# Two blocks of a layer pair on one core: new hand-laid queues, and 64x64 products that lie across the halves of two PSUM banks

## The chip, the core and the metric

The kernel runs on one core of a Trainium2 chip. Its time is that of the device in microseconds (us). Times that are compared are medians of several executions; a profile is of one execution, and has a time of its own.

## What is computed

The input is 2048 tokens of 512 features in bf16. Two kinds of block alternate, A B A B, each added to its input:

```python
def _A_ref(x, wqkv, wo):      # H = 32 heads of 16, window W = 256
    qkv = (x @ wqkv).reshape(B, S, 3, H, Dh)
    scores = einsum("bhqd,bhkd->bhqk", q, k) * Dh ** -0.5
    mask = (i - j >= 0) & (i - j < W)
    return einsum("bhqk,bhkd->bhqd", softmax(where(mask, scores, -1e9)), v) @ wo
def _B_ref(x, w1, b1, w2, b2):     # mixes tokens: F = 1792
    u = gelu(einsum("bsd,sf->bdf", layernorm(x), w1) + b1)
    return einsum("bdf,fs->bds", u, w2) + b2
x = x + _A_ref(_layernorm(x), A_wqkv, A_wo)
x = x + _B_ref(_layernorm(x), ...)        # and both once more
```

## The kernel before

**Stages.** A "layer" below is one A and one B; there are two. The attention of a layer is cut into four quarters Q of 512 queries, and a quarter into four groups t of 8 heads, and these into 9 steps m: 144 steps a layer, 288 in all. In a step TensorE multiplies scores (`emit_scores`, L753), ScalarE takes exp from two PSUM banks (`emit_exp`, L765, into one of ten slots of `p_all`), VectorE or GpSimd masks the window's edges (`mask`, L795), and TensorE multiplies with v (`emit_pv`, L816). Scores have two pairs of PSUM banks (0-1, 2-3) in turn, the sums with v have banks 4 and 5. After the ninth step the sums are copied out of banks 4 and 5 into `oU` and `o2` (`copy_out`, L374 on VectorE, L376 on ScalarE). After each second group two DMAs move rows of `o2` into `oU`, and two move the softmax denominators into `den_c`, so the next copy into `o2` waits for DMAs of the groups before. `job_inverse` and `job_normalise` (L842 to L867) divide, `job_outproj` (L726) multiplies with wo and adds to x.

**Work beside the attention.** The products with wqkv (`job_kq`, `job_v`), with wo, a part of the first product of B (`job_u_part`) and, in the first layer, twelve of the sixteen tiles of B's second product (`job_y_pair`) are put between the steps of attention. All go through `pair`, which makes two products at once in the two "misc" banks 6 and 7. Three kinds of work share these banks: pairs, `job_normalise`, and some of B's products. The bank of each use is read from the string `BANKS`. A digit of the string `CELLS` says how `pair` makes the two: 0 is each product as matmuls of 128x128 weights and 512 columns (L559), and 1 is both at once in four 64x64 tiles of TensorE (L573); then row half r works on product r, and on the other one in the second half of the pass, so that the row halves never write one bank at the same time. The attention's own matmuls are all 64x64 tiles. A stretch of 128x128 matmuls between 64x64 ones is called an island here.

**The rest of B** lies between the attentions: `u_product` and `job_u` (L944), `job_y` (L1035, L1022), with layer norm (`ln_stats` L488, `ln_apply` L508 to L520). Transposed inputs `xhT` (two buffers in turn) of the quarters after the first come by DMA transposes that SyncE issues (`job_transpose`, L535).

**Order.** `Plan.op` records each piece of work with its reads and writes, and so its dependencies. The order on each engine was searched off line and is written out: `ORDER` names, two letters an operation, what TensorE, VectorE, ScalarE, GpSimd and SyncE each run, one after the other. `arrange` reads it, lets users of one misc bank follow each other in TensorE's order, and `needs` sets the waits. Each engine runs its list strictly in order, SyncE (the DMA queue) too: what waits holds all that is behind it.

```python
        for b in sorted({int(s) for s in self.stays}):
            used = [self.res["bank", s].users for s in self.stays if int(s) == b]
...
            a, b = misc_bank(), misc_bank()
            pairs.append((a, b))
            if CELLS[len(pairs) - 1] == "0":
                for i, bank in enumerate((a, b)):
                    for lo, hi in pieces or ((0, n),):
```

Without `pieces`, a product of four matmuls is one operation, so nothing comes between its matmuls.

Of the kernel before, what the change touches and what calls it, by code (L numbers as in the profile page):

```python
# [7 lines left out]
ALU = mybir.AluOpType  # L8
# [7 lines left out]
CELLS = '000001000000110001001110000001000000000000000000000000000000001100000101000000'  # L16
# [13 lines left out]
        ApAqArAsAtBEAuBGAvBKBIBOBMBQBSAwAxB4CXCUBkCfCcDRCoCTClC2BlCuDAAyC8CeCkDLCnCtC1DGCyDZC7DVCxDhC-DEDIDeBuDmDrBvD5DPDYD8DSEH  # L30
        DdDgEKE+ERDlDqEUD4D7EAEjEmDuErEvDvEJEQETEiE5ElEqEuE0EzEYFVE2FCFxFdE9FaFpFyFiFBF2FUFZFtEZGDFcFhGAFoFsF1F5GPGlGHGCGZGLGWGG
        GOGVGhGYGcGdGmGxGgGpGqG+G7GuG4GKHPG-HJG3HXH3HTH4HmG6HIHjHOHSHzG0HWHiHlHwHpIEI8IBHyH2INIDIJHLIKIMIQItIRHaI2HbIxIcIwJBIVI6
        IzJIIUJFI9JYJMKvJiJcI5JnJjJAJxJEJHJLJ0JXJbJmJ4JqKAJ7KHJ8KKJzJ3J-KOKGKJKSKwKbKNKRKgMWKnKaKdKsLoK6LpLAKmKrLEK5KXLILUKWLXMX
        LhK-LDLkLHLTKjLyLWLaL1MQL5LjL8MPMALnL0MML4L7K8MUL-MLMTMdNJMaMhMsMjMwMkMzMgMrM3MvMyM2NDMDNHMENSNCNGNNNdNWNgLLNlLMNoNfNvNK
        NyNkN6ObN+MnNnOHOCNuNxN5N9OBOVN1OOOEOkN2OZONOUOYOuOjOoOpORO1OtOyMoPCOxO0O-OcPRO4PONPPePBPNPWOQPnPQPjNOP6PVPdP0PiOKPmPrQB
        P3P+PaQJPZQFP9QAQbQEOfQOQIQNQaQeRbQfQgPFPGRVRYPsPtRZRhRcQqReRiRfQtRSRTQ5QxRgQ4QwRWRURPRQRMRRRNRORoRXRmRqRaR0R1RdRsRwSARk
        RuSBR4SISESJR8R9R5SFRjRySwTtTuSxSmTvSnSrSsShSiTwTpTqTrTsUXS9UYTDUZS-UaTBTGTFTJTdTlTKUbT7T+UcUdUDUGUeThUTT9ULTiTTUyUCUFUK
        U2USUxU7TUU1U6VAU9VKUPVNUOVSVVVHVaVEVMVfVRVUVtVZVeVsVwVjV7VvV0V+WGVGWYWVWHWIWqWnWJWCWvWzV9WUWXWmWpW4WuWyW3W9WDWEW6XJXGWF
        ViXrXOXCXBXwXFXIX1XNXqXvX0X4X5XUYBYCYMWcXVYPYTX+XWYbYFYiXXX9YlYpYOYSYaYhYkYoYtXQY2YsZJY1ZGXRXSZTZQXTYxZPZSZnZhYWYXZrZgZm
        ZvWdZ7ZqZuZ6Z9Z+aBaIY8aLYyY9ayaKavY+Y-a5aka2Y4Y5a9bJY6Y7bNaxa1bSa4ZMbWa8bIbMbPbdZWbhbVbcbkZjbgbjbobnbYbZbzb3b0aOaPaQaRcB  # L40
        cAb4aSZXcLcOcEaTaUaVZycccUbBcYcmcjalb9b8cNcqZzcTcuc3cbcXc8ciclcpdDctc2c5dGbAdUdCdcamdgdFdTdkdJdwdbdfdjdzdKdvdyd9eAd2cyeO
        czeRd-eDeVeQeUeYeEeeeXeqeFeuezc-edepete3ewe+e5fefFe2fCe6fVe9fBfJg2fofEfZgLf2fIfUfzfYfhfsf+fdf7gIgMgFf1gUg3gQf6f9gEgdgHdW
        gYgPgTgXgtgagkdog8gjgxehhGgsgwhBdnhNhKeihag7hAhXhFgghJhMhphQhmh4hZhlhohthugmgnh9h3iBh8goiOgpiAiUiFiYiRfifjibiffkflijiXia
        ioieiiini1gzi0i4jvi5i6iGhzh0hej1hdj7iHjsjEj4jwjyjHj2j8jTjSj5jLjKjzjthxjmjnhyj3jojukIjpj9j+jxj0kGkCjqkijrkjkWkAkMkSkTkekf
        kEkOkPkXkakbj6kKlClGk2k3lDlHk6k7lOlSlPlTlelflalmlblql2lrlyl3lnlzlulvl6mFl7l+l-mC
    """,
    "vector": """
        A2ASATAQA3ARA0A1AUAVA8AWA6A4A7A5A+BAA-AXBFBDBCBUBJBYBZBaBRBWBVBXBbB8BcBeCWBmBoDTCVBqBnCaBrCrBjIfBtIdFGDDC0CzFEBsDKDbBxDp
        FIByIgFKDUIhFAECEWFHB1EoFJFFIjFLDxIiB2IeFMB3FOIkDyDzEyEaE3FzFXE-D1F0FrD2FSInFkFgF4EcF6F7EbGFFTEdGnIlGNGSGjEfGoHAGvGwGMHB
        HCHDHEGzHFH5H6HGHVG1G2HrHqI+IGHHHMHNH7H8H9ITHcHfHdH+I1IZIaIWI-IXKxHgHeIYHhIbJRKzJlJPJkJ2JrJsKCJ9K1KMJ+KDKUKyMYKeKfK2LqK3  # L50
        KuLrKZLsLGKEKYMZLZLuKlLbLcKkL3MSMRK+K9LvMONLMcMbMlMmLwM5MIMFMGNXNYMJLQLNMHLONMLRLPN0LSMKN8M8NrM6OdOAM+M-OFOGN3N4OwNsOTOr
        MqO6O5NROeOSPgNQPlOLP4OMP5PcPbQLOhQQOgQhPKPHQnPIPuPvPxQrPwQsPyPLPJPMPzQRQuQTQvQYQWQVQ9Q1Q+Q2Q6QyQ7Q3QzQ0Q-Q8RCRARGRER2SC
        SKR+R6SGSySzSoS0SpSqStSuSjSkSvSlS3S1T0TxTyS+TETATCUfTIT5UgTNTMTQUAToUhTST6UiUIUnUJUoTzTRUpTkUrUVTVTXUWTWU+U4URUQU5VXVJVc
        VdTZVhTaVyVlV1VIWNWbWsW-W8WKXLVkVmXMXDXzVoUvVpWSYEYAYRWTYGYHX-XbWLYrYeZHXgXYWMZVXhXZWgXaXkXiYYYZWiZtWhWfaCaDWjY0YfaNYga0
        WkWlXpZDZAbLZEZBZFZObQbRZNZkZlZabmbbaWaXcDZCZdcGcFaZaaZ0abaYaebFbGacceb-b+cfcoZ3cgapcZc6c7Z1bCaqaoZ2asdiZ4Z5bHbDdmbEbrdL
        aud3btd4d1dNc0c1dPdOdQeGeHegdRdAdBeIexe7bwfge8fAg4byfLfqgNftfuffgAgOg5gBgSdYdXgbgcdseLgCejekgDdtdueldpdqemendreofOfMghhc
        hSgifRfQfTeMhrh6iDeNh-gqiSiTiWidfnfmilg0iqg1i8i7iIh2hijBhjiJhfiLiKjFhgjGjIjJiMiNjXhhhkirjUitivjPjQjMjVjYjNjOjWjZjRjajcjh
        kkkUkQkYkgkclIlEk8k4lglUlclQlol0lwl4mGlsl8mAmD
    """,
    "scalar": """  # L60
        AaBHAcAbAdAzBLBPBNBTAlB5CYAfCgCdCpAoCmC3CvDBC9DMDHDaDWDiDfDJDnDsBwD6D9EIELESEVEkEnEBEwDwEsE6E1FWFDFeE4FbFqFjF3FuGEGBGQGI
        GaGXGiGeGyGrGTG8G5HQHKHYHUHnHkH0HxIFICIOILIuISI3IyJCI7JJJGI0JNJZJdJoJyJ1J5KBKIKLKPKTKcKhKoKtK7LBLFLJLVLYLiLlLzL2L6L9MBMN
        MVMeMiMtMxM0M4NENINTNeNhNmNpNwNzN7N-MpOIODOWOPOlOaOvOqO2OzPDPAPSPPPfPXPoPkP7P1QCP-QKQGQcQPRIQiQoQXRFRHRnRrRvRtR3RpRlRxSL
        SDR-R7SHRzS6SYS7THTLTeTmT8T-UHUETjUMUUUzU3U8VBVLVOU-VTVWVbVgVuVxV-V8TbWZWWV2WoWrWwW0W5W+XKXHW7XPXsXEXxX2X6YDYNWeYQYUYcYj
        YmYqYuZKY3ZIZUZRYzZiZoZsZwZ8Z-aJaMXnazawa6a3a+bKbObTbXbeZYbiblbpbab1cCb5ZZcPZfcMcdcVcaanckcncrcvc4c9dEdHdVdddhdldxd0dMd+
# [12 lines left out]
        FnO7O9O8OsPYO+NVOiOnPUQjQkKqSaPhQZRKQmQlSNIHSOQHRLSQPqNjP2QMSPRJKpSSSZSeSRSMSbSfSdSgUNScSTT2T1UkUjT3TgUlVFTfT4V3V6V4UmV5
        YIWPYLYKYJWQWOWRaEXeXcXfaFaGXdaHYVYwX8X7cHcKcIcxcRcJcSb7cWb6d5d8d6d7ecfvebfyfwfxhThVg-hWhUdZhEg6hwh7hsi+i9iEjji-frfbjAkm
        kqjkjlf5fcdak0kxizkvimk1kniQkzkrihkwkokskuktkpk9lMlLkylAk-lVk+lKlWlJljk5ldlXlYlhlklilBlNl5lZlRlxlllplFltl1l9mBmHmE  # L80
    """,
}
BANKS = (
    "7667766776766767666677767767666767767666677667677767767667676767677667676776766767767667677766677777"
    "7767766767766767776776676777667666676776676667776767767667677667776776667767666776677776676667676767"
    "7677"
)
# [24 lines left out]
class Plan:  # L112
# [52 lines left out]
    def arrange(self):  # L165
# [119 lines left out]
def bass_interleave_layers__sliding_block__mixer_token_mlp__prompt_kernel(  # L285
# [11 lines left out]
    S = A_x.shape[1]  # L297
# [12 lines left out]
    with es:  # L310
# [216 lines left out]
        def misc_bank():  # L527
            stays.append(Bank(BANKS[len(stays)]))
            return stays[-1]

# [18 lines left out]
        def pair(make, n, prio, reads, pieces=None):  # L549

            a, b = misc_bank(), misc_bank()
            pairs.append((a, b))
            if CELLS[len(pairs) - 1] == "0":
                for i, bank in enumerate((a, b)):
                    for lo, hi in pieces or ((0, n),):
# [8 lines left out]
            for half in range(2):  # L564
                for lo, hi in pieces or ((0, n),):
# [14 lines left out]
            return a, b  # L580

# [34 lines left out]
        def store_k(Q, t, b, prio):  # L616
            masked(b, prio, k_sb[:, Q % 2, t].rearrange("p b (h n) -> p b h n", h=2), ps[:, b, :].rearrange("p (b n) -> p b n", n=32),
                   half, "half", [R("k", Q % 2, t, hf) for hf in range(2)], 1226, 1230)

        def store_q(Q, t, b, prio):  # L620
            masked(b, prio, q_sb[:, t].unsqueeze(1), ps[:, b, :].unsqueeze(1), even, "even", [R("q", t)], 1226, 1230)
# [44 lines left out]
        def job_v(Q, i, prio):  # L666

            a, b = pair((w_half(Q, 2, 2 * i), w_half(Q, 2, 2 * i + 1)), 4, prio, w_held(2, 2 * i) + xhT_all(Q))
            for j, bank in enumerate((a, b)):
                copy_out(vT[:, j, :], ps[:, bank, :], bank, prio, 691, [R("vT", j)])  # L670
                plan.ops[-1].deps = dict.fromkeys(plan.ops[-1].deps, 0)
# [510 lines left out]
```

## Time and profile before

| | |
|---|---|
| median of 3 runs | 494.68 us (494.25 to 495.84) |
| the profiled execution | 493.93 us, its span 492.2 us |
| granted TensorE clock | 1.0 in every slice |
| attention of the first layer | from 13.71 us to about 155 us |
| B of the first layer | to about 229 us |
| attention of the second layer | 229.19 us to about 390 us |
| B of the second layer | to 488.9 us |
| busy in 60 to 80 us | PE 17.66, DVE 16.54, ACT 19.36, POOL 13.95 of 20 |
| busy in 420 to 440 us | PE 19.89, DVE 4.04, ACT 8.21, POOL 0 of 20 |

Times in the profile count from the start of the span. PE is TensorE's matmuls, PEld its weight loads, DVE VectorE, ACT ScalarE, POOL GpSimd, SP SyncE. A row of the timeline gives start, length, engine, line, operation, tiles and number of instructions merged, and in brackets how long the engine was idle before and who ended it. Some matmul records are missing: of an island of four, often three are shown.

### The profile page before, as it was taken

The numbers are of one execution on the slowest core, as the hardware profiler recorded it, in microseconds if no ns is written. First come the engines' busy times: TensorE is split into PE (matmuls) and PEld (weight loads), VectorE is DVE, ScalarE is ACT, GpSimd is POOL, SyncE is SP. The second block draws the span as 40 slices with busy tenths as digits, with TensorE's granted clock in tenths as the row PEclk, the third lists the DMA queues.
The fourth block names the chain that finished last, engine by engine and source line by source line (L and its number), as shares of the span: only waits on it lengthen the run. The fifth ranks groups of instructions, "written<-read, shape, count | busy, mean of one in ns | idle before, by whom it ended". The sixth has DMA issues, their size and how long they took to land.

```text
span 492.2 us, 17751 instructions
## 1 busy us (share of the span) xinstructions
PE 465.4 (95%) x7966; PEld 260.5 (53%) x8042; DVE 327.1 (66%) x623; ACT 316.2 (64%) x389; POOL 197.3 (40%) x270
## 2 busy tenths in 40 slices
PE   7999997999999999999999999999999999999997
PEld 6545563766655444443555556456557644444444
DVE  6999997998966741346856776689996674022213
ACT  3999997999997013306898899699999602330000
POOL 5998975736553100013654444286643003000000
PEclk9999999999999999999999999999999999999999
DMA  7231542603105980301510342062023497022553
GB/s 212 90 46 49 110 93 46 92 11 43 49 20 140 280 225 9 99 0 44 119 47 3 101 107 41 15 99 49 3 50 81 113 265 215 1 85 62 153 150 128
DMA packets 85180, 43.63 MB, mean 89 GB/s; under 512 B 19953, under 2 KB 84081, under 8 KB 85105
## 3 DMA queue, kind: packets, MB, share of 16 engines
q1 hardware_dynamic: 81232, 42.48, 33.7%
q0 software_dynamic: 3872, 0.02, 1.3%
q8 instruction: 63, 1.03, 0.9%
q14 instruction: 13, 0.10, 0.1%
HBM read 32.51 MB, written 2.10 MB: 70 GB/s over the span
## 4 chain that ended last, share of the span: by engine, by line
PE 58%; DVE 11%; ACT 11%; DMA 6%; POOL 5%; SPq 4%; issue 3%; DVEq 0%; POOLq 0%
PE ps L559 17%; PE ps L1035 12%; ACT p_all L765 10%; PE ps L944 10%; PE ps L753 8%; PE ps L816 6%; DMA oU<-o 4%; PE ps L573 3%; SPq L368 3%; DVE stats L488 2%; POOL p_all L795 2%; DVE q_sb L607 1%; POOL xh_sb L517 1%; SPq L535 1%; DMA k_sb<-in_B_w_dram 1%
## 5 line engine op out<-in xcount | busy, mean ns | idle before, releaser
L765 ACT ACTIVATE p_all<-ps 128x1024 bf16<-128x1024 f32 (+8 forms) x288 | 260.0, 974 | 21.2 <-PE ps L753 19.2
L795 POOL TENSOR_TENSOR p_all<-p_all,edge 128x512 bf16<-128x512 bf16 (+3 forms) x125 | 97.9, 790 | 102.9 <-ACT p_all L765 98.5
L753 PE MATMUL ps<-q_sb,k_sb 64*64 64x288 bf16 (+8 forms) x2816 | 107.1, 249 | 2.1 <-ACT p_all L765 1.6
L816 PE MATMUL ps<-p_all,v_all 64*64 64x288 bf16 (+8 forms) x2816 | 86.6, 246 | 1.2 <-DVE p_all L795 0.6
L753 PEld LDWEIGHTS ps<-q_sb,k_sb 64*64 64x64 bf16 x2816 | 56.1, 106 | 52.9 <-ACT p_all L765 32.5
L559 PE MATMUL ps<-xhT,wqkv 128*128 128x512 bf16 x281 | 73.4, 380 | 9.9 <-issue 4.0
L816 PEld LDWEIGHTS ps<-p_all,v_all 64*64 64x64 bf16 x2816 | 58.7, 107 | 10.1 <-issue 3.3
L1054 DVE SCALAR_TENSOR_TENSOR x_sb<-ps,b2col,x_sb 128x512 bf16<-128x512 f32 x31 | 22.7, 746 | 56.4 <-PE ps L1035 46.5
L559 PEld LDWEIGHTS ps<-xhT,wqkv 128*128 128x128 bf16 x320 | 25.9, 97 | 38.3 <-issue 4.6
L510 POOL TENSOR_TENSOR rstd<-vare,mhalf 128x4 f32<-128x4 f32 x15 | 15.3, 1022 | 76.5 <-DVE vare L508 73.4
L488 DVE BATCH_NORM_STATS2 stats<-x_sb 128x6 f32<-128x512 bf16 x64 | 42.8, 681 | 4.1 <-DMA x_sb<-in_A_x_dram 3.6
L559 PE MATMUL ps<-uT,w1buf 128*128 128x512 bf16 x157 | 39.0, 380 | 1.5 <-issue 1.4
L520 ACT ACTIVATE xh_sb<-x_sb,shift,rstd 128x512 bf16<-128x512 bf16 x9 | 7.1, 809 | 51.7 <-POOL shift L514 51.7
L656 POOL TENSOR_TENSOR v_all<-vB,evens 128x512 bf16<-128x512 bf16 x29 | 33.9, 1172 | 14.5 <-DVE vB L674 13.9
L607 DVE TENSOR_TENSOR q_sb<-ps,even 128x1024 bf16<-128x1024 f32 x29 | 35.1, 1213 | 5.7 <-PE ps L559 5.5
L795 DVE TENSOR_TENSOR p_all<-p_all,edge 128x128 bf16<-128x128 bf16 (+3 forms) x87 | 29.6, 345 | 12.8 <-ACT p_all L765 11.5
L607 DVE TENSOR_TENSOR k_sb<-ps,half 128x1024 bf16<-128x1024 f32 (+1 forms) x28 | 33.4, 1194 | 2.0 <-PE ps L559 1.5
L1035 PE MATMUL ps<-uT,oU 128*128 128x512 bf16 x151 | 34.4, 379 | 0.2
L1007 DVE TENSOR_TENSOR v_all<-v_all,ps 128x512 f32<-128x512 f32 x12 | 8.2, 687 | 39.3 <-PE ps L944 39.3
L944 PE MATMUL ps<-xh_sb,k_sb 128*128 128x512 bf16 x124 | 30.0, 379 | 1.6 <-DMA k_sb<-in_B_w_dram 0.9
L867 DVE TENSOR_TENSOR oT<-oU,ps 128x512 bf16<-128x512 f32 x32 | 21.2, 680 | 9.7 <-PE ps L860 7.5
L559 PE MATMUL ps<-wo_sb,oT 128*128 128x512 bf16 x99 | 24.9, 380 | 1.2 <-issue 0.6
(98 smaller groups left out, 543.6 us busy)
## 6 DMA issues: line engine op xcount, KB each, us to landing
w1buf<-in_B_w_dram SPq DMA_DIRECT2D x50, 256.0 KB, 3.6
oU<-in_B_w_dram SPq DMA_DIRECT2D x18, 256.0 KB, 5.0
oU<-o SPq DMA_DIRECT2D x32, 128.0 KB, 3.2
k_sb<-in_B_w_dram SPq DMA_DIRECT2D x16, 256.0 KB, 4.6
q_sb<-in_B_w_dram SPq DMA_DIRECT2D x8, 256.0 KB, 5.6
xhT<-in_B_w_dram SPq DMA_DIRECT2D x8, 256.0 KB, 4.9
out_dram<-x_sb SPq DMA_DIRECT2D x15, 128.0 KB, 1.8
x_sb<-in_A_x_dram SPq DMA_DIRECT2D x5, 256.0 KB, 2.8
```

What stands on the lines that cost most here:

```text
L488: dve(lambda e: e.bn_stats(stats[:, t % 8, :], x_sb[:, t, :]), 697, prio, reads=[R("x", t)], writes=[R("stats", t % 8)])
L559: last = e.matmul(ps[:, bank, :], lhsT=lhs(None), rhs=rhs, start=(k == 0), stop=(k == n - 1))
L607: return e.tensor_tensor(dst, src.unsqueeze(2).to_broadcast([P, n, 2, w]), mask[:].unsqueeze(1).unsqueeze(3).to_broadcast([P, n, 2, w]), o ...
L656: return e.tensor_tensor(spots, src.unsqueeze(3).to_broadcast([P, 8, 2, 2, DH]), evens.rearrange("p (h d) -> p h d", h=2).unsqueeze(1).uns ...
L753: last = e.matmul(ps[64 * c:64 * c + 64, 2 * half + r, 32 * i0:32 * i1], lhsT=k_sb[rows, ring, t, kb % 16, :], rhs=q_sb[rows, t, c, 32 * i ...
L765: latest[0] = in_table(plan.op({ACT: (180 + int(2 * (512 - c0) * 0.832), lambda e: e.activation(p_sb[:, slot, :, c0:512], ps[:, 2 * half:2 ...
L795: return e.tensor_tensor(v, v, g, op=ALU.mult)
L816: last = e.matmul(ps[64 * r:64 * r + 64, B_O + (c ^ r), 32 * i0:32 * i1], lhsT=v_sb[rows, t, vn, vk, 32 * r:32 * r + 64], rhs=p_sb[rows, s ...
L867: dve(lambda e, t=t, b=b: e.tensor_tensor(oT[:, buf, t, :], oU[:, buf, t, :], ps[:, b, :], op=ALU.mult), 693, prio, reads=held_o(buf, t), ...
L944: r = e.matmul(ps[:, b, :], lhsT=blk[:, n, (ft % 2) * P:(ft % 2 + 1) * P], rhs=xh_sb[:, 4 * g + n, :], start=(first and g == quarters[0] a ...
L1035: r = e.matmul(ps[:, b, :], lhsT=blk[:, fc, (st % 2) * P:(st % 2 + 1) * P], rhs=uT[:, fc, :], start=(fc == 0), stop=(fc == NFT - 1))
L1054: dve(lambda e: e.scalar_tensor_tensor(x_sb[:, st, :], ps[:, b, :], b2col[:, st:st + 1], x_sb[:, st, :], op0=ALU.add, op1=ALU.add), 754, prio,
```

## The change

`CELLS` has five letters now. With a, b or c the first, the second or both products of a pair are made alone in 64x64 tiles (`across`): the product's 512 columns lie half in bank 6 and half in bank 7, row half r works on one half of the columns and then on the other, in matmuls of 256 columns. Such a product holds both misc banks until it has been read. Seventeen products are made so: eleven of 4 steps along the contraction, one of 8, five of 14. Pairs of kind 1 go from 12 to 5. A product of 4 matmuls is now two operations of 2, between which others can come. `ORDER`, `BANKS` and `CELLS` come from a new search, whose clock counts the fetching of each block of instructions; that clock is no part of the kernel. No other function changes what it does; readers take the bank through `held_in`.

```diff
-CELLS = '000001000000110001001110000001000000000000000000000000000000001100000101000000'
+CELLS = '00010000a00b00ba00100b0000001abb00000000000001bb0c000c0b000000000b00010a000000'
...
-        ApAqArAsAtBEAuBGAvBKBIBOBMBQBSAwAxB4CXCUBkCfCcDRCoCTClC2BlCuDAAyC8CeCkDLCnCtC1DGCyDZC7DVCxDhC-DEDIDeBuDmDrBvD5DPDYD8DSEH
+        ApAqArAsAtBEAuBGAvBKBIBOBMBQBSBmBnBkCdB8BlCZClCaCXCiCuAwDZCYC+CrDaAxC0AyDIDECkC3C4DOCqCtDTC5C6DfCzC9DDDjDHDMDQDoBwDrBxDb
...
-        for b in sorted({int(s) for s in self.stays}):
-            used = [self.res["bank", s].users for s in self.stays if int(s) == b]
+        for b in (6, 7):
+            used = [self.res["bank", s].users for s in self.stays if int(s) in (b, -1)]
...
+        middle = ps.rearrange("p b n -> p (b n)")[:, 6 * 512 + 256:7 * 512 + 256]
...
-            a, b = misc_bank(), misc_bank()
+            kind = CELLS[len(pairs)]
+            a, b = misc_bank(kind in "ac"), misc_bank(kind in "bc")
             pairs.append((a, b))
-            if CELLS[len(pairs) - 1] == "0":
+            pieces = pieces or ((0, n // 2), (n // 2, n))
+            if kind != "1":
                 for i, bank in enumerate((a, b)):
-                    for lo, hi in pieces or ((0, n),):
+                    if int(bank) == -1:
+                        across(make[i], bank, len(pieces) // 2, n, prio, reads)
+                        continue
+                    for lo, hi in pieces:
...
+        def across(make, bank, parts, n, prio, reads):
+            before = None
+            for swap in range(2):
+                for part in range(parts):
+                    lo, hi = n * part // parts, n * (part + 1) // parts
+                    def f(e, swap=swap, lo=lo, hi=hi):
+                        for k in range(lo, hi):
+                            for r in range(2):
+                                rows, side = slice(64 * r, 64 * r + 64), slice(256 * (r ^ swap), 256 * (r ^ swap) + 256)
+                                lhs, rhs = make(k, rows)
+                                for c in range(2):
+                                    last = e.matmul(middle[64 * c:64 * c + 64, side], lhsT=lhs(c), rhs=rhs[:, side],
+                                                    start=(swap == 0 and k == 0), stop=(swap == 1 and k == n - 1),
+                                                    skip_group_check=True, tile_position=(64 * r, 64 * c))
+                        return last
+                    o = pe(f, 444 * (hi - lo) // 4, prio, reads=reads, writes=[BK(bank)], mode="cells")
```

Some operations change their engine with the new order. Of the copies of `o2`, VectorE has 21 and ScalarE 11 (26 and 6 before); of the 64 spreads of v, VectorE 41 (33 before); of the mask operations, VectorE 73 and GpSimd 139 (87 and 125). DMAs are the same 237, in another order.

More of the change, by code (lines that the diff above doesn't have):

```diff
@@ L34 @@
[L34 to L41, printed above, removed]
@@ L564, in pair @@
             for half in range(2):
-                for lo, hi in pieces or ((0, n),):
+                for lo, hi in pieces:
                     def f(e, half=half, lo=lo, hi=hi):
@@ L580, in pair @@
             return a, b
+        def across(make, bank, parts, n, prio, reads):
[14 more added lines that the diff above has]
+                    o = pe(f, 444 * (hi - lo) // 4, prio, reads=reads, writes=[BK(bank)], mode="cells")
+                    if swap and not part:
+                        o.deps[before] = -1
+                    before = o
         def strip(c, at=0):
@@ L725, in job_outproj @@
                 tile = 4 * Q + i
-                dve(lambda e, b=b, tile=tile: e.tensor_tensor(x_sb[:, tile, :], x_sb[:, tile, :], ps[:, b, :], op=ALU.add), 693, prio,
+                dve(lambda e, b=b, tile=tile: e.tensor_tensor(x_sb[:, tile, :], x_sb[:, tile, :], held_in(b), op=ALU.add), 693, prio,
                     reads=[R("x", tile)], shares=[BK(b)], writes=[R("x", tile)])
@@ L973, in job_u_part @@
                          sum((w1_place(j, q)[1] for q in quarters), []) + [R("xh", sc) for q in quarters for sc in range(4 * q, 4 * q + 4)],
-                         [(k, k + 4) for k in range(0, n, 4)])
+                         [(k, k + 4) for k in range(0, n, 4)] if n > 4 else None)
             for ft, b in zip((2 * j, 2 * j + 1), banks):
```

104 lines of the change are left out of this document (58 added, 46 removed).

## The prediction

> **What bounds the kernel now.** I read the page first, then TensorE's waits, then the timeline around the longest of them.
>
> ```profile
> PE 465.4 (95%) x7966; PEld 260.5 (53%) x8042; DVE 327.1 (66%) x623; ACT 316.2 (64%) x389; POOL 197.3 (40%) x270
> ...
> q8 instruction: 63, 1.03, 0.9%
> ...
> PE 58%; DVE 11%; ACT 11%; DMA 6%; POOL 5%; SPq 4%; issue 3%; DVEq 0%; POOLq 0%
> ```
>
> TensorE is busy 95% of the span, and it alone has more than half of the chain that ended last. So I count its time in three parts: streaming, mode switches, waits. One step of streaming is the time from one matmul's start to the next: 216 ns for 512 columns, 109 to 110 ns for four 64x64 tiles of 256 columns, 123 ns for four of 288 (medians over the trace). Summed over the program this is 438.1 us. A switch shows here:
>
> ```profile
> 112.42 0.39 PE L753 MATMUL ps<-q_sb,k_sb 64*64 64x64 bf16 x12
> 112.97 0.81 PE L559 MATMUL ps<-xhT,wqkv 128*128 128x512 bf16 x3 [0.16 <-issue]
> 113.71 0.41 PE L816 MATMUL ps<-p_all,v_all 64*64 64x256 bf16 x8
> ```
>
> The last round before this island starts at 112.58 and takes 0.07 (160 columns). The four matmuls take 4 x 0.216 = 0.863 (the fourth has no record). The next tiles start at 113.71: 113.71 - 112.58 - 0.07 - 0.863 = 0.197 us too late. Of some 110 islands nearly all give 0.196 to 0.198. With 111 islands the switches cost 21.9 us. 438.1 + 21.9 = 460.0, so some 32 us of the span are the start (first score at 13.71, with 8 us of work before it), the end (3.3 us) and waits. The waits by releaser begin so:
>
> ```profile
> PE ps L559 <- issue: 6.7, 42, 0.2
> PE ps L559 <- DVE x_sb L726: 3.0, 2, 2.7
> PE ps L753 <- ACT p_all L765: 1.6, 4, 0.6
> ```
>
> The first row is the switches. The second is one wait of 2.7 us. Its cause stands in two timelines:
>
> ```profile
> 70.48 5.18 SPq L535 DMA_TRANSPOSE xhT<-xh_sb  x3
> 75.71 1.98 SPq L368 DMA_DIRECT2D oU<-o  x2
> ```
>
> ```profile
> 79.78 0.69 DVE L374 COPY o<-ps 128x512 f32<-128x512 f32 x1 [2.62 <-DMA oU<-o]
> ...
> 81.34 0.81 PE L559 MATMUL ps<-xhT,wqkv 128*128 128x512 bf16 x3 [2.73 <-DVE x_sb L726]
> ...
> 82.77 1.02 ACT L765 ACTIVATE p_all<-ps 128x1024 bf16<-128x1024 f32 x1 [2.54 <-PE ps L753]
> ```
>
> SyncE issues three transposes before the two DMAs that empty `o2`. VectorE's next copy into `o2` stands at the head of its list and waits 2.62 us. Behind it is the read of a misc bank (L726), TensorE waits for that bank, and ScalarE then waits 2.54 us for scores: all engines stand.
>
> ScalarE sets a floor in the first layer: six exps in a row take 5.70 us, so a quarter's 36 take 34.3. From the first exp of the second quarter (47.33) to that of the third (85.00) there are 37.7 us, with 0.9 of other ScalarE work; the 2.5 us of the wait are nearly all of the rest. The two quarters after it take 35.0 and 34.3: no room.
>
> **The change part by part.**
>
> 1. *Streaming and switches.* The built program has 8704 matmuls (8042 before) and 109 islands (111). Halves of products make 24 islands of only two matmuls, and this eats what the products across two banks save. Each of those products' 122 contraction steps takes 2 x 109.1 = 218.1 ns instead of 215.7: +0.3 us. Switches: -2 x 0.197 = -0.4. Together -0.1 us, on the path, as TensorE is. That 256 columns keep pace is shown by the attention's own 256-column rounds.
>
> 2. *Instruction blocks.* 662 more matmuls with as many weight loads are 1324 instructions; 63 packets hold some 16,200, so 5 more. A packet takes about 1 us. Bounds: 0 if it is read ahead, +5 us if each is waited for. In 63 packets the trace has one gap within attention without a semaphore (0.19 us, at 66.78), so I take 0. The Trainium skill, "Runtime: NRT & Kernel Launch", Instruction fetch mechanics, says that the sequencer reads the next block while it runs this one, so that a crossing is mostly hidden. The trace agrees. The rule speaks against the change: a clock that counts fetches would be counting what costs nothing.
>
> 3. *The wait at 78.4.* In the new order of SyncE the first of the two `o2` DMAs stands ahead of all four transposes, the second behind one. That transpose needs a tile that VectorE now makes after the masks of step 57, about 70 us; with 1.3 to issue it, 0.6 for the DMA and 3.35 to land, `o2` is free near 75.5. The copy that waited is on ScalarE now, behind the exp of step 69, near 82. So -2.6 us; bounds 0 (another wait takes its place) and -2.73. Late next are the other three transposes: GpSimd makes their last two tiles after the mask of step 65 (near 77), they are issued by about 84 and land by 86, and the first product that reads them comes near 88.
>
> 4. *Two smaller waits.* The first product with v waits 0.60 for a mask on VectorE (22.58); the products with wqkv for v that feed the queue there now come before the first score: -0.3 (0 to -0.6). At 332.17 a product waits 0.39 for transposes; it now comes four steps (some 4 us) later: -0.4 (0 to -0.4).
>
> 5. *Between the layers.* TensorE waits at the first product with wqkv:
>
> ```profile
> 225.87 1.90 PE L559 MATMUL ps<-xhT,wqkv 128*128 128x512 bf16 x8 [0.52 <-DVE xhT L374]
> ```
>
> A piece of 0.65 us now stands between the last transpose and it: -0.5. But the first piece of the next `job_y_pair` takes a bank one transpose (0.22) after the product that held it ended, and the read of that bank takes 0.75 (L1054) and 0.16 for the matmul's tail (380 ns long, 216 apart): +0.7. Together +0.2 (-0.5 to +0.7).
>
> 6. *The start.* VectorE gets a 0.74 us copy of ones (such a one is at 14.27) ahead of the second tile's statistics, on the way to the first transpose; VectorE has gaps there: +0.3 (0 to +0.74). TensorE's three half products (1.3 us) before the first score replace the warm-up that ran there from 12.50 (1.28).
>
> 7. *Held banks.* For every user of a misc bank I took its distance on TensorE from the user before, in streaming time, and from it the read's duration (copy 0.68, x 0.75, q and k 1.21) and 0.15. Before, 31 distances have less than 0.3 us to spare, and the short ones miss 0.9 us in all. After, 54 have, and they miss 2.4. Without the 0.7 of point 5 that is +0.8; the worst is a normalisation in the quarter that ScalarE bounds, so I take +0.4 (0 to +0.8).
>
> Work that moves to ScalarE (three copies more by count, at 0.60) falls mostly into the second layer and the ends, where it has gaps. DMAs are 237 in both.
>
> Sum: -0.1 + 0 - 2.6 - 0.7 + 0.2 + 0.3 + 0.4 = -2.5 us. The profiled execution took 493.93 (span 492.2 and 1.73 around it): 491.4. It lies 0.75 below the median of the runs, 494.68; against that median I forecast **492.2**. Bounds of the terms added up: -4.3 to +7.1, the upper one nearly all from the fetches and the wait at 78.4.
>
> **Rivals.** *a) The time saved is eaten again.* The stretch after 78 is bound by ScalarE, and a quarter's floor of 34.3 stays. If the three late transposes miss their product by 2 us, the wait only moves: 494.7, no change. For it: their slack is 2 us. Against it: it needs GpSimd to be later than its place says. *b) Held banks decide, slower.* The 23 additional tight distances are all in lists that run in order; if VectorE is late by 0.25 us at each (waits of this kind now are 0.3 to 0.5: `PE ps L559` on q_sb 0.8 in 2, on oT 0.6 in 2), that is +5.7 and the sum +3.2: 497.9. It decides, to slower, from 0.17 us each. Against it: many of these waits would fall where TensorE waits for ScalarE anyway. *c) More is gained.* Halves fit between scores where a whole product (0.86 and a switch) was longer than an exp (0.95); if this ends half of the 14 us that TensorE loses between one tile round and the next (the 2.6 is not in it), the sum is near -7: 487.7. Against it: there are as many islands as before, and in the quarters of 34.3 to 35.0 us ScalarE has nothing to give.
> *d) Weight loads bound the new products.* Four loads a round take 106 ns each in the trace; one after the other they would be 424 against 109, and 244 rounds would cost +77 us: 571. But the attention's rounds have the same four loads and keep 110. The Trainium skill, "TensorEngine Tiling (Array Packing)", Restrictions, says that column tiling disables fast weight loads. No round here shows that this sets the pace.
>
> **Chances.** The forecast (490 to 493.2) 0.45; a) 0.21; b) 0.20; c) 0.13; d) 0.01. A change under 0.3% (1.5 us) can hardly be told from none. Faster: the forecast and c), 0.58; same: a), 0.21; slower: b) and d), 0.21. The range from 488.0 to 497.5 leaves out the ends of b) and c).
>
> **What would show it.** Point 3: no gap over 1 us on all engines between 70 and 90 us, and a quarter from the second's first exp to the third's near 35.2. Point 1: islands still 0.197, the new rounds 109 ns apart. Point 2: 68 packets and no new gaps without a semaphore. Point 5: 0.7 on x_sb (L1088 there) before the second attention. Rival b) would show as more `PE <- DVE` waits of 0.2 to 0.5 us. The forecast is wrong if such waits add up to over 2 us, or if the wait at 78.4 comes back at another DMA.

## The result, and the profile after

The changed kernel takes **492.23 us** (median of 8, 491.43 to 493.85), the kernel before beside it 495.86 (494.25 to 497.58): ratio 0.993, interval 0.9906 to 0.9953. Measured again (e3): 493.12 against 495.89, ratio 0.9946 (0.9925 to 0.9968). So it is faster, by 2.7 to 3.6 us, and the forecast of 492.2 met the time. The sum behind it did not hold in all its terms, and the median it was taken from, 494.68, lies 1.2 below the one beside the changed kernel.

The page of the changed kernel (TensorE first, then the instruction packets, then the chain of waits):

```profile
PE 466.8 (95%) x8633; PEld 274.2 (56%) x8704; DVE 326.2 (66%) x616; ACT 318.9 (65%) x392; POOL 196.8 (40%) x274
...
q8 instruction: 68, 1.11, 0.9%
...
PE 76%; DVE 11%; POOL 4%; issue 4%; ACT 2%; DMA 2%; SPq 1%; POOLq 0%
```

68 packets, as counted. TensorE's share of the chain rises from 58 to 76%: less of the time is other engines' now. TensorE's waits by releaser (total, times, longest):

```profile
PE ps L571 <- issue: 5.8, 35, 0.5
PE ps L850 <- DVE p_all L829: 1.7, 2, 1.2
PE ps L467 <- POOL ident L403: 1.4, 1, 1.4
PE ps L850 <- issue: 1.3, 3, 0.5
PE ps L787 <- issue: 1.0, 2, 0.8
...
PE ps L571 <- DVE x_sb L1088: 0.6, 1, 0.6
```

The 2.7 us on `x_sb` are gone; the 0.6 at L1088 are those of point 5. The rows with "issue" on L850 and L787 are longer than any that the two profiles of the kernel before have on these products (0.4 at most); nothing that the profile shows was waited for there. The timeline around 78 us (start, length):

```profile
74.06 0.59 SPq L370 DMA_DIRECT2D oU<-o  x1
...
78.59 4.36 SPq L542 DMA_TRANSPOSE xhT<-xh_sb  x3
...
79.46 0.59 ACT L378 ACTIVATE o<-ps 128x512 f32<-128x512 f32 x1
...
80.18 0.81 PE L571 MATMUL ps<-xhT,wqkv 128*128 128x512 bf16 x3 [0.16 <-DVE p_all L829]
```

The second `o2` DMA is issued 4.5 us ahead of the three transposes, the copy into `o2` on ScalarE starts without a wait, and the longest pause marked at a matmul between 74 and 81 us is 0.16. So point 3's mechanism is as forecast. But a second profile of each kernel was taken. The table gives when an exp on ScalarE starts (us), by the number of exps that ScalarE has run before it, so that about equal work lies behind each row. The rows are near the starts of the quarters: the exp of step 36 comes after 37 others in both orders. In the changed order the exps of steps 0, 108 and 144 come one place later than before, behind those of steps 1, 109 and 145, and so a comparison step by step would find those three 0.9 to 1.1 us later than the work is.

| exps before | before | before, 2nd | changed | changed, 2nd |
|---|---|---|---|---|
| 0 | 14.18 | 13.65 | 13.32 | 13.17 |
| 37 | 47.33 | 46.10 | 46.76 | 46.57 |
| 72 | 85.00 | 83.69 | 82.25 | 82.48 |
| 108 | 120.00 | 118.69 | 118.45 | 118.36 |
| 144 | 229.79 | 228.82 | 228.13 | 227.70 |
| 180 | 265.15 | 264.17 | 263.10 | 262.66 |
| 217 | 311.44 | 310.47 | 309.06 | 310.00 |
| 253 | 352.82 | 351.73 | 351.18 | 352.15 |
| span | 492.2 | 490.9 | 490.6 | 492.1 |

The stretch from 37 to 72 exps, the second quarter, is 1.9 us shorter on the mean, the quarter after it 1.0 longer, and the spans differ by 0.2. Profile against profile almost nothing is gained. The two profiled executions of the kernel before took 493.93 and 492.67, which is among its fastest: of 109 others only 20 are below 493.93, and half lie above 495. The gain of the medians is for a good part in executions that are longer than the profiled ones. Each run lists its mean granted clock: 29 of those 109 have 0.997 or less and take 497.2 on average, the other 80 take 494.8. All 20 of the changed kernel have 0.999 or 1.0, and so have all 60 of the runs below that are made from it (e4 to e7, e10). That is 0.6 us of the difference of the means; where the clock is lost is shown under e2. The other 80 are still 2.0 us above the mean of the changed kernel's 20 (492.8), and no kept trace shows an execution of the kernel before that is as long as most of them.

For what follows I took every two successive matmuls on TensorE from the first score to the end and subtracted the streaming step (us; the borders of instruction blocks are shown under e10). The rows are not all: gaps of under 0.03 us between two operations, some 7 us in each of these profiles, are in none.

| | before | before, 2nd | e1 | changed | changed, 2nd | e4 | e6 | e10 |
|---|---|---|---|---|---|---|---|---|
| switches (islands x 0.197) | 20.9 | 20.9 | 20.9 | 20.7 | 20.7 | 29.0 | 18.5 | 20.7 |
| waits for semaphores in the attentions | 13.4 | 12.2 | 11.5 | 10.8 | 10.2 | 8.9 | 17.0 | 10.6 |
| the same, at a block's border | 0.6 | 0.4 | 0.7 | 2.1 | 3.1 | 0.1 | 3.1 | 1.6 |
| gaps at a block's border, no semaphore | 0.2 | 0.6 | 0.6 | 2.8 | 3.9 | 1.4 | 2.4 | 6.5 |
| waits in B | 3.2 | 3.0 | 3.0 | 2.1 | 2.1 | 2.1 | 2.1 | 2.1 |

### The profile page after: what moved, and what is told of

Its sections match the earlier page's. It is cut to its first block, busy times and chain, and to the rows that moved or that the text cites. A ratio compares the mean times of both kernels' runs of the same rounds, so it can differ in the third digit from the quotient of the medians.

```text
span 490.6 us, 19076 instructions
## 1 busy us (share of the span) xinstructions
PE 466.8 (95%) x8633; PEld 274.2 (56%) x8704; DVE 326.2 (66%) x616; ACT 318.9 (65%) x392; POOL 196.8 (40%) x274
## 4 chain that ended last, share of the span: by engine, by line
PE 76%; DVE 11%; POOL 4%; issue 4%; ACT 2%; DMA 2%; SPq 1%; POOLq 0%
PE ps L571 21%; PE ps L978 15%; PE ps L1069 12%; PE ps L787 10%; PE ps L850 9%; PE ps L607 5%; ACT p_all L799 2%; PE ps L585 2%; DVE stats L490 2%; PE ps L894 1%; DVE k_sb L641 1%; DVE q_sb L641 1%; POOL p_all L829 1%; DMA w1buf<-in_A_wqkv_dram 1%; DVE v_all L690 1%
## 5 line engine op out<-in xcount | busy, mean ns | idle before, releaser
L799 ACT ACTIVATE p_all<-ps 128x1024 bf16<-128x1024 f32 (+6 forms) x288 | 259.6, 977 | 19.6 <-PE ps L787 17.9
L829 POOL TENSOR_TENSOR p_all<-p_all,edge 128x512 bf16<-128x512 bf16 (+3 forms) x139 | 107.0, 778 | 110.4 <-ACT p_all L799 108.6
L787 PE MATMUL ps<-q_sb,k_sb 64*64 64x288 bf16 (+8 forms) x2816 | 106.9, 249 | 1.9 <-issue 1.0
L850 PE MATMUL ps<-p_all,v_all 64*64 64x288 bf16 (+8 forms) x2816 | 87.0, 246 | 3.1 <-DVE p_all L829 1.7
L787 PEld LDWEIGHTS ps<-q_sb,k_sb 64*64 64x64 bf16 x2816 | 56.0, 106 | 49.6 <-ACT p_all L799 32.7
L571 PE MATMUL ps<-xhT,wqkv 128*128 128x512 bf16 x283 | 75.2, 381 | 6.3 <-issue 3.6
L850 PEld LDWEIGHTS ps<-p_all,v_all 64*64 64x64 bf16 x2816 | 59.8, 107 | 11.4 <-issue 4.0
L1088 DVE SCALAR_TENSOR_TENSOR x_sb<-ps,b2col,x_sb 128x512 bf16<-128x512 f32 x31 | 22.6, 747 | 64.1 <-PE ps L1069 49.9
L571 PEld LDWEIGHTS ps<-xhT,wqkv 128*128 128x128 bf16 x320 | 24.6, 97 | 34.0 <-issue 5.6
L571 PE MATMUL ps<-wo_sb,oT 128*128 128x512 bf16 x110 | 29.2, 380 | 1.8 <-issue 1.1
L829 DVE TENSOR_TENSOR p_all<-p_all,edge 128x512 bf16<-128x512 bf16 (+3 forms) x73 | 25.7, 357 | 7.0 <-ACT p_all L799 6.6
L760 DVE TENSOR_TENSOR x_sb<-x_sb,ps 128x512 bf16<-128x512 bf16 x32 | 21.6, 681 | 10.7 <-PE ps L571 10.1
L690 POOL TENSOR_TENSOR v_all<-vB,evens 128x512 bf16<-128x512 bf16 x21 | 24.8, 1185 | 8.4 <-DVE vB L708 6.7
L901 DVE TENSOR_TENSOR oT<-oU,ps 128x512 bf16<-128x512 f32 x32 | 20.7, 681 | 8.3 <-PE ps L894 7.3
```

The lines of the kernel that those rows point to most:

```text
L571: last = e.matmul(ps[:, bank, :], lhsT=lhs(None), rhs=rhs, start=(k == 0), stop=(k == n - 1))
L690: return e.tensor_tensor(spots, src.unsqueeze(3).to_broadcast([P, 8, 2, 2, DH]), evens.rearrange("p (h d) -> p h d", h=2).unsqueeze(1).uns ...
L787: last = e.matmul(ps[64 * c:64 * c + 64, 2 * half + r, 32 * i0:32 * i1], lhsT=k_sb[rows, ring, t, kb % 16, :], rhs=q_sb[rows, t, c, 32 * i ...
L799: latest[0] = in_table(plan.op({ACT: (180 + int(2 * (512 - c0) * 0.832), lambda e: e.activation(p_sb[:, slot, :, c0:512], ps[:, 2 * half:2 ...
L829: return e.tensor_tensor(v, v, g, op=ALU.mult)
L850: last = e.matmul(ps[64 * r:64 * r + 64, B_O + (c ^ r), 32 * i0:32 * i1], lhsT=v_sb[rows, t, vn, vk, 32 * r:32 * r + 64], rhs=p_sb[rows, s ...
```

## The experiments

**before_again**, the kernel before once more.

> The kernel before, unchanged, for a second profile. If its executions differ by DMA times, the first scores of the steps 36, 72, 108 and 144 lie within 0.3 us of those of the first profile (46.57, 84.53, 119.47, 229.19), except where a wait for a DMA is longer or shorter; the wait at 78.4 us of 2.6 us comes again. If the wait of 2.6 us is an accident of one execution, it is absent here.

492.67 us. The exps of steps 36 to 144 lie 1.0 to 1.3 earlier than in the first profile, so not within 0.3. Of this 0.5 is from the start, and most of the rest is the wait of 0.60 for a mask at 22.58 (point 4), which is absent here: on VectorE the spread of v ahead of that mask takes 0.81 us, and 1.38 in the first profile. Waits for DMAs nearly cancel:

```profile
56.01 1.02 PE L559 MATMUL ps<-xhT,wqkv 128*128 128x512 bf16 x4 [0.67 <-DMA xhT<-xh_sb]
...
79.81 1.04 PE L559 MATMUL ps<-xhT,wqkv 128*128 128x512 bf16 x4 [1.49 <-DVE x_sb L726]
```

The wait at 78 us is there again, but 1.5 us long instead of 2.7, and at 55 us there is one for a DMA transpose that the first profile did not have. So what stands behind SyncE's transposes differs between these two executions.

**e1_sync_order**: in SyncE's list, after a DMA of denominators (`Hs`), the two `o2` DMAs (`Hv`, `Hu`) go ahead of the three transposes.

```diff
-HsJhKVJgHvHu
+HsHvHuJhKVJg
```

> The kernel before with one change in SyncE's list: the two DMAs that empty o2 at about 74 us stand ahead of the last three DMA transposes of that quarter, not behind them. My theory (point 3): the wait of 2.6 us at 78.4 goes, the third quarter's first exp comes near 82.5 (85.00 before), and as ScalarE's quarters after it have no room to give, nearly all of it stays: 492.0 to 492.6 against 494.7, about -2.2 us (ratio 0.995 to 0.996). Rival a): the time is eaten again by the end of the attention, by ScalarE or late transposes: the first exp of step 144 within 0.5 us of 229.8, ratio 0.999 to 1.001.

493.05 us, ratio 0.9953 (0.9927 to 0.9979): -2.3 us. SyncE, and then VectorE and TensorE at that place:

```profile
72.43 1.21 SPq L368 DMA_DIRECT2D oU<-o  x2
73.68 5.16 SPq L535 DMA_TRANSPOSE xhT<-xh_sb  x3
```

```profile
77.60 0.69 DVE L374 COPY o<-ps 128x512 f32<-128x512 f32 x1
...
79.05 1.04 PE L559 MATMUL ps<-xhT,wqkv 128*128 128x512 bf16 x4
```

No bracket: nothing waits. The first exp of step 72 comes at 82.93, the quarter from step 36 takes 36.2 us for 37.6, and the one from 72 to 108 takes 35.0 as before: nothing is given back there. By the medians my theory holds and a) does not: one swap in one queue gives most of what the whole change gives. Profile against profile it is less clear. The first exp of step 144 is at 228.30, 1.5 us ahead of the first profile of before but only 0.5 ahead of the second, and the span of 490.5 is 1.7 and 0.4 shorter.

**e2_split256**: many more instructions in the old order.

```diff
-    last = e.matmul(ps[:, bank, :], lhsT=lhs(None), rhs=rhs, start=(k == 0), stop=(k == n - 1))
+    for h in range(2):
+        cols = slice(256 * h, 256 * h + 256)
+        last = e.matmul(ps[:, bank, cols], lhsT=lhs(None), rhs=rhs[:, cols], start=(k == 0 and h == 0),
+                        stop=(k == n - 1 and h == 1), skip_group_check=True)
```

> The kernel before with each 512-column matmul of the products in 128x128 tiles made as two of 256 columns with the same weights: 656 matmuls and as many weight loads more, 1312 instructions, as many as the change adds, and 5 fetched blocks more; order and waits are the same. My theory (fetches are read ahead, point 2): 656 x 2.4 ns of streaming = +1.6 us at most, ratio 1.001 to 1.004. Rival (each fetch is waited for, about 1 us): +6.6 us, ratio 1.013, and gaps without a semaphore in TensorE's stream, five more than before or one at each block.

Ratio 1.0022 (0.9998 to 1.0046), +1.1 us: the rival's +6.6 is out, my +1.6 is inside. That fetches are all read ahead does not follow: two gaps without a semaphore (0.60 and 0.74 us) are at borders of blocks. The profiled execution was a long one (499.06), and shows where the clock goes. First TensorE's wait, then the stretches around it (length, busy time and instructions of PE, PEld, DVE, ACT, POOL, then granted clock, DMA share, GB/s):

```profile
57.86 1.06 PE L561 MATMUL ps<-xhT,wqkv 128*128 128x256 bf16 x8 [1.99 <-DMA xhT<-xh_sb]
```

```profile
55.00:57.80 2.80, 0.87 (x40) 0.60 (x32) 1.99 (x4) 2.29 (x4) 2.75 (x4) 1.00 0.27 50
57.80:58.80 1.00, 0.94 (x8) 0.71 (x8) 0.00 (x0) 0.00 (x0) 1.00 (x2) 0.97 0.98 221
58.80:62.10 3.30, 3.30 (x43) 2.05 (x43) 1.98 (x3) 1.94 (x2) 1.06 (x3) 0.50 0.81 251
62.10:66.00 3.90, 3.90 (x85) 2.49 (x88) 3.66 (x7) 3.13 (x4) 2.33 (x6) 0.99 0.01 4
```

TensorE stands for 2 us, goes on at full clock for 1 us, and then has half its clock for 3.3 us: 1.65 us lost, 0.997 as a mean over 497. That is the value which the long executions show.

**e3_after_again**, the changed kernel as a base for the next three: 493.12, ratio 0.9946 (0.9925 to 0.9968).

> The changed kernel itself, beside the three that are made from it, as their base: ratio to the kernel before 0.990 to 0.996, as in the first runs.

**e4_held_whole**: the 17 products as plain matmuls in the same places.

```diff
-                            for r in range(2):
-                                rows, side = slice(64 * r, 64 * r + 64), slice(256 * (r ^ swap), 256 * (r ^ swap) + 256)
...
+                            lhs, rhs = make(k, slice(0, P))
+                            last = e.matmul(ps[:, 6, :], lhsT=lhs(None), rhs=rhs, start=(k == 0), stop=(k == n - 1))
```

> The changed kernel with its 17 products across two banks made as plain 128x128 matmuls of 512 columns in bank 6, in the same places of the order, and still holding both misc banks: only tile mode and instruction count differ (7850 matmuls for 8704, some 7 fetched blocks fewer), and islands rise from 109 to 151. My theory (switches are paid, fetches are not): 42 x 0.197 - 0.3 = +8.0 us if all lies on the path, +5 to +8 as some switches fall into TensorE's waits. Rival (the fetches count): 7 us of it are won back, so +1. Rival (the gain of the change does not come from the products across banks but only from the order): below +2.

495.32, +2.2 us against e3. My +5 to +8 fails, the rival with the fetches is near. The table shows why: 42 islands more cost 8.3, but gaps at borders fall by 2.5, waits at borders by 3.0, other waits by 1.3. This run cannot tell fewer instructions from borders that lie at other work.

**e5_one_bank**: as e4, each product in one bank (and some other digits in `BANKS`).

```diff
-CELLS = '00010000a00b00ba00100b0000001abb00000000000001bb0c000c0b000000000b00010a000000'
+CELLS = '000100000000000000100000000010000000000000000100000000000000000000000100000000'
```

> As e4_held_whole, but each of the 17 products holds one misc bank only (the one that the next user does not need). The difference to e4_held_whole is the price of holding two banks. My theory (point 7): -0.4 us for the change's share, 0 to -1 against e4_held_whole. Rival b) (held banks decide): -3 to -5.7 us against e4_held_whole.

494.71, 0.6 less than e4 on the same chip by the medians, and 1.3 by the ratios (0.9976 for 1.0002). Rival b) is out.

**e6_joined**: in TensorE's list 41 first halves of products go to just ahead of their second halves, so (`Bk`, `Bl`, with two scores between):

```diff
-BkCdB8Bl
+CdB8BkBl
```

> The changed kernel with the two halves of each product of four matmuls next to each other again: 41 first halves are moved to just ahead of the second; the islands fall from 109 to 98. My theory (halves make islands, and these eat what the products across banks save): -11 x 0.197 = -2.2 us against the changed kernel, at most +1 where a whole product between two scores makes ScalarE wait. Rival c) (the halves fit between scores, and that is where time is gained): slower, +2 to +8 us: some 28 of the 41 have scores between their halves, and a block that is 0.43 us longer makes ScalarE wait up to 0.3 at each.

498.25: +5.1 against e3, so my -2.2 has the wrong sign, and c)'s mechanism is right: 11 islands fewer, but TensorE waits for ScalarE ten times, and ScalarE for scores 44 times instead of 34:

```profile
PE ps L787 <- ACT p_all L799: 3.5, 10, 0.5
```

```profile
ACT p_all L799 <- PE ps L787: 22.3, 44, 1.2
```

In the changed kernel the latter row reads so:

```profile
ACT p_all L799 <- PE ps L787: 17.9, 34, 1.2
```

The new order needs its halves. That does not make halves worth 5 us against the old order, which e1 shows to be nearly as fast without them.

**e7_mask_ahead**: two moves in the changed kernel at its 1.2 us wait for a mask: the mask (`GX`) ahead of a transpose (`Et`) and a store of k on VectorE, a score (`Gx`) ahead of half a product (`HW`) on TensorE.

```diff
-EtG+GX
+GXEtG+
...
-HWGx
+GxHW
```

> The changed kernel with two moves at 52 us, where its TensorE waits 1.2 us for a mask that stands on VectorE behind a copy, a transpose and a store of k: the mask goes ahead of the transpose, and one score (step of exp at 55.4) goes ahead of the first half of a product that waits for VectorE. My theory (a quarter bound by ScalarE keeps what ScalarE does not wait for): the exp that started at 54.44 starts near 53.3, and 0.5 to 1.1 us stays to the end, ratio to the kernel before 0.9915 to 0.9935 where the changed kernel had 0.993 and 0.9946. Rival a) (eaten again): the wait comes back at the blocks of eight matmuls at 109 to 115 us, 0.

Ratio 0.9942 (0.992 to 0.9964), no different from the changed kernel. ScalarE and TensorE in e7, and then the same place in the changed kernel:

```profile
49.01 5.61 ACT L799 ACTIVATE p_all<-ps 128x1024 bf16<-128x1024 f32 x6
...
53.74 0.63 PE L607 MATMUL ps<-xhT,wqkv 64*64 64x256 bf16 x16 [0.49 <-DVE vT L376]
...
54.74 0.41 PE L850 MATMUL ps<-p_all,v_all 64*64 64x128 bf16 x12 [0.37 <-DVE p_all L829]
```

```profile
49.53 3.77 ACT L799 ACTIVATE p_all<-ps 128x1024 bf16<-128x1024 f32 x4
...
53.75 0.42 PE L850 MATMUL ps<-p_all,v_all 64*64 64x64 bf16 x12 [1.16 <-DVE p_all L829]
...
54.44 1.94 ACT L799 ACTIVATE p_all<-ps 128x1024 bf16<-128x1024 f32 x2 [1.13 <-PE ps L787]
```

Six exps run in a row instead of four, and then ScalarE's pause comes two exps later: counted from the first exp of step 36 they start at 4.60, 5.50, 6.40, 7.31, 9.85 (changed kernel: 4.60, 5.50, 7.68, 8.60, 9.71). VectorE had the same work to do first. It is rival a), within 3 us and not at 109.

**e8_sync_and_late_v**: e1, and on TensorE the product that waits at 55 us (`G+`) behind two scores, a product with v and the next product (`GK`).

```diff
-G+G7GuG4GKHP
+G7GuG4GKG+HP
```

> e1_sync_order and one move more: the first product with v of the second quarter, for which TensorE waited 0.67, 0.75 and 1.99 us at a DMA transpose in three of four profiles of this order, stands behind the product that followed it. My theory: the rest of the change's gain over e1_sync_order is this wait and the half clock that can follow a wait of 2 us: median 0.2 to 1.0 us below that of e1_sync_order (493.05), and no run with a mean clock of 0.997 or less, where the kernel before has 18 of 57 and e1_sync_order 2 of 11. Rival: the clock falls for another reason, and 2 of 11 stay.

Ratio 1.0037 (1.0015 to 1.0058), 3 to 4 us slower than e1, and 2 of 12 executions at 0.997 or less. My theory fails here: the wait for the DMA is gone from the list, but the copies of that product come later, and others wait for them:

```profile
PE ps L860 <- DVE oT L867: 1.3, 2, 0.7
PE ps L573 <- DVE vT L374: 1.1, 1, 1.1
PE ps L559 <- DVE vT L374: 1.0, 2, 0.6
```

What lets the clock fall in these two stays open.

**e9_longer_wait**: the kernel before with a load of weights (`II`) ahead of the two `o2` DMAs.

```diff
-HvHuJfII
+IIHvHuJf
```

> The kernel before with a load of weights moved ahead of the two DMAs that empty o2, so that the wait at 78.4 us is 0.6 to 1.0 us longer (3.2 to 3.6 us). My theory (point 3, the wait lies on the path): +0.6 to +1.0 us, ratio 1.001 to 1.002 without more falls of the clock; if the wait at 78.4 is also what lets the clock fall, more runs than 18 of 57 show a mean clock of 0.997 or less and each of them costs 2.2 more. Rival (the time is eaten again, ScalarE sets the pace): 0.

```profile
75.39 2.31 SPq L368 DMA_DIRECT2D oU<-o  x2
...
79.48 0.69 DVE L374 COPY o<-ps 128x512 f32<-128x512 f32 x1 [2.69 <-DMA oU<-o]
80.83 1.04 PE L559 MATMUL ps<-xhT,wqkv 128*128 128x512 bf16 x4 [2.58 <-DVE x_sb L726]
```

The wait is 2.58 us in this profile, between the 1.49 and the 2.73 of the two profiles of the kernel before; that it is longer on the whole is not shown by it. Ratio 1.0061 (1.0032 to 1.009), +3.0 us, more than the 0.6 to 1.0 of my theory; the rival's 0 is out. Six of 12 executions have a clock of 0.997 or less (two 0.992) and average 498.8, the other six 495.8. Of the kernel before beside it these are 6 of 29 (496.4) and 23 (494.3). So the moved load costs about 1.5 us where the clock is kept too, which fits a wait on the path but is more than it was to be. That the clock falls oftener is as expected, but 6 of 12 against 6 of 29 can be chance.

**e10_shifted** and **e11_sync_shifted**. The "issue" rows were still open. In every trace the program's TensorE instructions can be counted up to each gap without a semaphore: of those from 0.1 us up all but three lie 194 to 199 instructions after a multiple of 256, and start again 1.05 to 1.6 us after the end of an instruction packet of q8. (The three, 0.11 to 0.16 us, are in e2 and e11; two of them fall into the half clock.) One of the changed kernel's:

```profile
342.94 0.64 PE L894 MATMUL ps<-rc,spread 64*64 64x128 bf16 x32
343.39 0.24 PE L787 MATMUL ps<-q_sb,k_sb 64*64 64x128 bf16 x2
344.46 0.37 PE L787 MATMUL ps<-q_sb,k_sb 64*64 64x128 bf16 x8 [0.83 <-issue]
```

A group of 12 matmuls stops after its first rounds; the packet before it ran from 342.01 to 343.10. To shift the borders and nothing else, warm-up matmuls ahead of the first score are changed (here 5 rounds of four tiles and 4 whole ones; e11, made from e1, has 3 and 6):

```diff
-        def warm(e):
-            for _ in range(10):
+        def warm(e, full=10, rounds=0):
+            for _ in range(rounds):
+                for r in range(2):
+                    for c in range(2):
+                        e.matmul(ps[64 * c:64 * c + 64, B_O + r, 0:P], lhsT=ident[64 * r:64 * r + 64, 64 * c:64 * c + 64],
...
+            for _ in range(full):
                 last = e.matmul(ps[:, B_O, 0:P], lhsT=ident[:], rhs=ident[:], start=True, stop=True)
...
+            pe((lambda e: warm(e, 4, 5)) if n < 5 else warm, 1070 if n < 5 else 558, -7.2, reads=[R("ident")],
```

> The changed kernel with 140 instructions more on TensorE before the first score: of the first five warm-up groups, of ten dummy matmuls each, six matmuls are replaced by five rounds of four 64x64 tiles, in about the same time, while TensorE has nothing else to do. All later work and its order are the same, only the borders of the blocks of 256 instructions lie 140 instructions earlier in it. My new theory (the gaps without a semaphore that the changed kernel has at 298, 344 and 388 us are fetches that come too late, and the new order is laid around the borders): the gaps stand at the same place of the blocks again (195 instructions after a multiple of 256) but at other work, and by the time that each block's work takes their sum grows by about 3 us (blocks under 3.2 to 3.4 us: 5.1 to 8 for 1.9 to 5): ratio to the kernel before 0.998 to 1.002 where the changed kernel had 0.993 and 0.9946. Rival (the gaps belong to the work at those places): they stay at the same matmuls, and the time stays within 0.7 us.

495.33, ratio 1.0013 (0.9989 to 1.0037): by the ratios 3.3 to 4.1 us slower than the changed kernel, with the same work in the same order. The group from above now runs in one piece:

```profile
344.77 0.42 PE L793 MATMUL ps<-q_sb,k_sb 64*64 64x128 bf16 x12
```

and there are nine gaps at other work, 6.4 us in all, again at 194 to 199. The longest:

```profile
391.45 0.30 PE L856 MATMUL ps<-p_all,v_all 64*64 64x256 bf16 x4 [1.34 <-issue]
```

New theory right, rival out: the gaps belong to the borders of the blocks, not to the work there, and with the borders elsewhere the gain of the change is gone. The profiles show where: the first score is no later (12.61 for 12.88 and 12.73), but from 253 exps to the end e10 takes 141.8 us, the changed kernel 139.4 and 140.0. In that stretch lie 3.5 us of e10's gaps and 0.75 and 1.0 of the changed kernel's. The kernel before was not run with a shift, so it is not shown that a shift costs nothing else.

> e1_sync_order (the kernel before with the two DMAs ahead of the transposes) with 80 instructions more on TensorE before the first score, made in the same way (four dummy matmuls of each of five groups replaced by three rounds of four tiles). By the time that each block's work takes, no block is left that is under 3.2 us (1.9 us too late in sum before the shift, of which 1.3 us are seen as gaps at borders). New theory: -0.5 to -1.3 us against e1_sync_order, ratio to the kernel before 0.9925 to 0.9945 where e1_sync_order had 0.9953, so as good as the changed kernel or better. Rival: the same as e1_sync_order.

The gaps at borders without a semaphore are gone (0 for 0.6). The time is not better: 494.55, ratio 0.9985 (0.9953 to 1.0018), executions from 491.21 to 498.17. By the medians that is 1.5 us above e1, so my -0.5 to -1.3 fails. In the profiled one (495.05) a copy into `o2` waits at another place, behind two transposes that took 3.58 us to issue, where e1's took 3.26:

```profile
59.73 0.69 DVE L374 COPY o<-ps 128x512 f32<-128x512 f32 x1 [0.86 <-DMA oU<-o]
...
150.88 0.69 DVE L374 COPY o<-ps 128x512 f32<-128x512 f32 x1 [1.77 <-DMA oU<-o]
```

So the old order has the same conflict of SyncE's transposes with `o2` a second time, in the quarter's first third; e1 mends only the other. The second row is a wait of another copy into `o2` that the old order has in these profiles too (1.00 and 0.91 in the kernel before, 1.06 in e1); at 1.77 us TensorE waits 1.08 behind it. At 301.97 TensorE waits 1.42 more for VectorE's copy into `o2`. The changed kernel's profiles have no such wait of a copy into `o2`. In the changed kernel the transposes in question are issued from 37.6 to 45.3 us, ahead of it.

## Why the prediction was right, point by point

1. *Streaming and switches, -0.1.* Right: switches 20.7 for 20.9, and 0.19 to 0.21 each. But e4 shows that a saved island isn't 0.197 us saved: 42 more of them were 2.2 us in time, as other gaps fell.
2. *Instruction blocks, 0 (to +5).* **This step failed.** I took 0 because the trace of before had one such gap of 0.19, and did not ask whether the blocks of the new order run in less time. Measured: gaps at borders of 2.8 and 3.9 us for 0.2 and 0.6, +2.9 on the mean, and 2.1 more where a semaphore came due at a border too. The Trainium skill, "Runtime: NRT & Kernel Launch", Instruction fetch mechanics, has the fetch hidden behind the block that runs; here it isn't, where a block of 256 instructions runs in less time than its successor takes to come (last section), and the measurement decides. I read the rule as one against a clock that counts fetches; e10 shows that it matters for this order where the borders lie.
3. *The wait at 78.4 us, -2.6.* Mechanism right; in e1 it is worth 2.3 us. It is 1.5 and 2.7 long in the two profiles. In the changed kernel the quarter after it gives 1.0 back: TensorE's streaming and switches from 72 to 108 exps rise from 34.0 to 34.4 and 34.6 us, with 14 islands for 11, among them products of eight matmuls at 109.9 and 113.9 between scores. That is a) in part, by work moved there and not by late transposes. The quarter before it is also less tight than I put it: 47.33 is the start of ScalarE's 38th exp, so 35 exps, not 36, lie between it and 85.00.
4. *Two smaller waits, -0.7.* Both waits are gone, the gain is not found: the first 37 exps take 0.6 us longer, and those from 217 to 253 0.8 longer. The first wait is absent in the second profile of before too; the changed kernel has one of 0.5 for a mask at 29 us instead, and one of 1.2 at 53.7.
5. *Between the layers, +0.2.* The wait on `x_sb` (0.6) is there as forecast, yet the stretch from 108 to 144 exps is 0.45 shorter; waits in B fall by 1.0. I had not counted these.
6. *The start, +0.3.* Wrong in sign: TensorE's first score starts at 12.88 and 12.73 for 13.71 and 13.19, 0.65 earlier on the mean, and ScalarE's first exp as much. The first scores of the two kernels, before and changed:

```profile
13.71 0.62 PE L753 MATMUL ps<-q_sb,k_sb 64*64 64x288 bf16 x16
```

```profile
12.88 0.62 PE L787 MATMUL ps<-q_sb,k_sb 64*64 64x288 bf16 x16
```

7. *Held banks, +0.4.* About right: 0.6 (by the ratios 1.3) between e4 and e5, for plain products in these places.

So that the median came out at 492.2 is in good part luck. A term was too low by 3 (fetches) and 1.0 was given back; against this stand gains that were not in the sum: 0.65 at the start, 1.0 in B, 0.4 between 144 and 180 exps. Profile against profile these leave 0.2 us of the forecast 2.5. The rest of the gain of the medians is in executions of the kernel before that are longer than its two profiled ones: 0.6 us of it is lost clock, and what makes up the rest is not settled, as a long execution was profiled only in e2.

## What to carry to other kernels

In a queue that runs in order, look at what stands behind slow entries of uncertain length: one swap there gave 2.3 us by the medians, most of what a new search of all queues gave (with the borders shifted, in e11, 0.7 was left, and that is within the noise). Count the instructions too: a round of four 64x64 tiles is eight instructions, so 32 rounds are a block, and at 109 ns a round that is 3.5 us, less than a late fetch took here (2.0 + 1.1 + 1.3); a block of narrower rounds takes less still. And if only the median moves and the profiles do not, profile a long execution. Take a second profile, and all the runs, before a difference below 1% is read from one trace.

## What the runs showed of the hardware

*Late instruction blocks.* In the traces a packet of q8 begins up to 2.4 us after TensorE passed the border before (386.94 and 384.51 in the second profile of the changed kernel), lasts about 1.1, and after a gap TensorE goes on about 1.3 us behind its end. A block of 2.50 us of work, whose packet began at 1.07, was followed by a gap of 1.02 (changed, at 344.46); one of 2.44, whose packet began at 0.13, by 0.02 (before, 2nd, at 147.8); one of 3.76, whose packet began at 2.00, by 0.75 (changed, at 387.8). The longest gap, 1.5, is in e10. What makes a packet begin late is not settled.

*Half clock after a short wait.* In e2, 2 us without a matmul were followed by 3.3 us at a granted clock of 0.50; in the first profile of before the clock stayed at 1.00 after 2.7 us at 78.4. The Trainium skill, "TensorE: Matmul & The Clock Gate", Part 1, gives a window of about 3.4 us, and a fall to half after an idle one. The length agrees with 3.3; the wait does not, as it was only 2 us long here, and the measurement decides. Why 2 us were enough in one execution and 2.7 were not in another is open.
